# Summing v for eight blocks of queries in one go, with the exponentials' extra room taken from a third buffer of split weights

## The chip, the cores and the metric

The kernel runs on one core of one Trainium2 chip. The metric is the device time in microseconds (us) of one execution. The kernel before takes 845.59 us, the median of three runs (845.48 to 845.86).

## The reference

What must be computed, for x of 2048 rows by 512 columns in fp32, is a gated sum of two mixers:

```python
g = sigmoid((x * gate_w).sum(-1))
a = Re(DFT over the sequence of (DFT over the columns of x))   # Cr @ (x Wr') - Ci @ (x Wi')
b = softmax(q k' / 4, keys at most 255 rows back) v, 32 heads of 16 columns, then @ wo
out = g * a + (1 - g) * b
```

## The kernel before

**Two kinds of work share TensorE.** One is a stream of dense products of 128x128 weights by 512 columns: first the projections to v, q and k, then the transform over the columns (x by wi and by wr, the tile `dab`), and last, from about 300 us on, the transform over the sequence (`dc`, line 529), whose weights cr and ci come from memory in 64 pieces. Every fp32 operand of these is split into a high part `hi` (a cast) and a low part `lo` (the rest), and each product is three matmuls (hi by hi, hi by lo, lo by hi). The other kind is attention: 128 blocks of 64 queries (four groups of eight heads, 32 blocks to a group), and in each block four pairs of heads.

**The order on TensorE is written by hand** in the loop at the end of the kernel (L1020 to L1070). For each block n and each pair p it puts down: `s_pair(n, p)`, the scores (L367); a few matmuls of the dense stream (`fill`); `t_pair(k, p)`, the transposed scores of the block k = n - 19 (L449); and the dense stream again. From t, ScalarE makes exponentials (L450) into a tile PT of one block, and GpSimd zeroes what lies outside the window (L454, L458). `pv(j)` (L475) sums v with block j's exponentials: sixteen or more small matmuls, each recorded twice since fp32 takes two passes. It isn't done block by block but in *visits*: when k is at least a certain number of blocks ahead of `summed`, or at the end (k == 128), `pv` runs for all blocks from `summed` to k, and the t of that half step comes behind it. The number is 4 while the dense stream projects, and 6 once `more` is set, which happens when the projections are done ("proj"). So there are nine visits of four blocks, fifteen of six and a last one of two: 25. The other engines' order is found by the scheduler, with hints.

**Where the exponentials lie.** The pool tile `pt` has four buffers of a block each. Once `more` is set, two blocks in six go to `home` instead, a tile of 3072 columns into which projections were evicted before (`hl_tile`).

**What a visit reads and frees.** v is spread out for the matmuls by GpSimd (`v_spread`, L432) into two buffers `vpad0` and `vpad1` of four blocks each, from `vr` (one buffer), which a DMA on SyncE (SP) fills. A finished strip of 512 queries is scaled out of PSUM by VectorE (`o_out`, L496) and stored to `o_scr`.

**Pieces of cr and ci.** `Pieces.get` starts a piece: it queues the split of the next piece and loads the raw weights of the one after that, 512 KB on SP. A piece lasts 24 `dc` matmuls, and its four split jobs (L588: cast, low part, twice) are put down after the 3rd, 9th, 15th and 21st of them. `hi` and `lo` have three buffers in the pool `st`.

**The tail.** When the last visit is done, `attention_done` (L834) takes the space of `home` for a tile `rt` and that of vpad0 and vpad1 for two tiles `oraw`. The rest is the output projection by wo, in pairs of row blocks, put between the last `dc` matmuls by `tail_step` (L766): for a pair i, `wo_load` reads attention's rows back from o_scr into two `oraw` tiles, `wo_sums` makes sums on GpSimd (L876 to L879), `wo_split` splits them on ScalarE and VectorE (L80, L85), `wo_begin` starts the products (L922) with a copy on ScalarE (L931) and additions on VectorE (L933, L926), and `wo_end` finishes them. `rt` holds rows of the sequence transform, read back from `r_scr`. All loads are issued on SP, in the order of its program.

Of the kernel before, what the change touches and what calls it, by code (L numbers as in the profile page):

```python
# [32 lines left out]
def fnet_window_mix(ctx: ExitStack, tc: tile.TileContext, xT, x, wqk, wv, wr, wi, cr, ci, wo, gw, out):  # L33
    nc = tc.nc

    const = ctx.enter_context(tc.tile_pool(name="const", bufs=1))
    big = ctx.enter_context(tc.tile_pool(name="big", bufs=16))
    st = ctx.enter_context(tc.tile_pool(name="st", bufs=3))
    ev = ctx.enter_context(tc.tile_pool(name="ev", bufs=5))
    at = ctx.enter_context(tc.tile_pool(name="at", bufs=2))  # L40
    ps_a = ctx.enter_context(tc.tile_pool(name="ps_a", bufs=4, space=PSUM))
# [50 lines left out]
            mark("dve", nc.vector.scalar_tensor_tensor(lo, ps, scale, f(hi), op0=OP.mult, op1=OP.subtract))  # L92

    HALVES = slice(0, 512), slice(512, 1024)

    def load_raw(src):
        raw = st.tile([P, 1024], F32, name="raw", bufs=2)
# [1 line left out]
        return raw  # L99

    def split_raw(raw, act=False):
        hi = st.tile([P, 1024], F32R, name="hi")
        lo = st.tile([P, 1024], F32R, name="lo")
        for c in HALVES:
            split(hi[:, c], lo[:, c], raw[:, c], act)
        return hi, lo
# [2 lines left out]
    ended = []  # L109

    def split_soon(raw):
        hi = st.tile([P, 1024], F32R, name="hi")
        lo = st.tile([P, 1024], F32R, name="lo")
        for c in HALVES:
            jobs.append(lambda c=c: late(nc.scalar.copy if FIN else (nc.vector if masks else nc.gpsimd).tensor_copy,
                                         hi[:, c], raw[:, c]))
            jobs.append(lambda c=c: late((nc.vector if masks else nc.gpsimd).tensor_sub, lo[:, c], raw[:, c], f(hi[:, c])))
        return hi, lo

    def job(n):  # L120
        if n == 2 and ended:
            ended.pop(0)()
        if n % 6 == 3 and jobs:
            jobs.pop(0)()

    def load_split(src, act=False):
# [19 lines left out]

    with tc.manual_schedule(engines={mybir.EngineType.Activation, mybir.EngineType.DVE, mybir.EngineType.SP}):
        wraw, *xraw = [pt_raw() for _ in range(3)]
        wq0 = [st.tile([P, 1024], F32R, name=h) for h in ("hi", "lo")]
# [71 lines left out]
    gl = const.tile([P, 16], F32, name="gl")  # L221
    g1 = const.tile([P, 16], F32, name="g1")
    g0 = const.tile([P, 16], F32, name="g0")
    gwb = []

    GX = {}
# [10 lines left out]
    def gate(tb):  # L237
        t = GX[tb // 2][:, HALVES[tb % 2]]
        nc.vector.scalar_tensor_tensor(t, t, 1.0, gwb[0], op0=OP.mult, op1=OP.mult,
                                       accum_out=gl[:, tb:tb + 1])  # L240
        if tb == 15:
            e = const.tile([P, 16], F32, name="ge")
# [5 lines left out]
    TERMS = ((0, 0), (0, 1), (1, 0))  # L248


    home = const.tile([P, 3072], F32R, name="home")
    turn = iter(range(99))

    def hl_tile():
# [156 lines left out]
    V2 = {}  # L411
    PT = {}
    more = []

    VR = {}

# [19 lines left out]
    def t_pair(n, p):  # L436
        q0 = n % NB * BQ
        w = min(WIN, S - q0)
        if p == 0:
            if "proj" in have:  # L440
                more.append(n)
            c = (n - more[0]) % 6 * NP * WIN if more else 3072
            if c + NP * WIN <= 3072:
                PT[n] = f(home[:, c:c + NP * WIN].rearrange("p (a b) -> p a b", a=NP))
            else:
                PT[n] = at.tile([P, NP, WIN], F32, name="pt", bufs=4)
        pt = PT[n]
# [76 lines left out]
    def c_part(w, chunks, ab, ps, ends):  # L524
        for i in chunks:
            if FIN and i % 2 == 0:
                tail_step()
            for n, (a, b) in enumerate(TERMS):
                nc.tensor.matmul(ps, w[a][:, i % 8 * 128:i % 8 * 128 + 128], ab[SC[i]][:, b],  # L529
                                 start=i == ends[0] and a + b == 0, stop=i == ends[1] and a == 1)  # L530
                job(i % 8 * 3 + n + 1)
                if i != chunks[-1] or a == 0:
                    yield

# [46 lines left out]
        yield  # L581


    have = set()

    def late(fn, *args):
        with behind("act", "dve"):
# [7 lines left out]
    def dense():  # L595
# [83 lines left out]
        for sb in range(16):  # L679
# [7 lines left out]
            if sb in (5, 7):  # L687
                pieces.load()
            if sb == 11:
                pieces.split()  # L690
        for sc in range(4):
            ab[sc] = load_ab(0, sc)
# [328 lines left out]
    for n in range(N + LAG + 1):  # L1021
# [10 lines left out]
        for p in range(NP):  # L1032
            if n < N:
                s_pair(n, p)
            fill(n)
            visit = p == 0 and (k - summed >= (6 if more else 4) or k == N)
            if 0 <= k < N and not visit:
                t_pair(k, p)
            if p == 0:
# [73 lines left out]
```

## Time and profile before

| | |
|---|---|
| median of 3 runs | 845.59 us |
| the profiled execution | 845.1 us |
| its span, first to last instruction | 843.3 us |
| outside the span | 1.8 us |
| granted TensorE clock | 1.000 |
| TensorE (PE) busy | 838.5 us, 99% |
| VectorE (DVE) busy | 643.8 us, 76% |
| ScalarE (ACT) busy | 611.1 us, 72% |
| GpSimd (POOL) busy | 298.8 us, 35% |
| moved by DMA | 161.03 MB, mean 191 GB/s |

A row of a timeline gives the start in us from the span's start, the duration, the engine, the line, the operation, the tile written and those read, the form, and how many instructions the row holds; in brackets stands the idle time ahead of it and who ended it. The ends of matmuls are modelled, so of TensorE the starts are to be compared. A row of the table by windows gives a stretch, its length, then the busy time and number of instructions of PE, PE's weight loads, DVE, ACT and POOL, then the granted clock, the mean busy share of the 16 DMA engines, and GB/s.

### The profile page before, as it was taken

Reading aid. Unit: us, or ns where it says so; the run is one execution under the profiler, and the core shown is the slowest. Engines: PE = TensorE matmul, PEld = TensorE weight load, DVE = VectorE, ACT = ScalarE, POOL = GpSimd, SP = SyncE. Lnnn points to the kernel's source line nnn. Section 1 sums busy time; section 2 is a strip of 40 time slices with the busy share of each in tenths; the row PEclk is TensorE's granted clock in tenths of the full one; section 3 lists DMA queues with packets and bytes.
Section 4 is the critical chain, followed back from the end, with each engine's and each line's share of the span. In section 5 each row is a group of like instructions: output and inputs, shape, how many; then the busy total and the mean of one; then the engine's idle time right before and its main releaser. Section 6 shows DMA issues by size and latency. Waiting matters only on the chain.

```text
span 843.3 us, 17171 instructions
## 1 busy us (share of the span) xinstructions
PE 838.5 (99%) x5310; PEld 695.8 (83%) x5310; DVE 643.8 (76%) x2083; ACT 611.1 (72%) x1832; POOL 298.8 (35%) x606
## 2 busy tenths in 40 slices
PE   9999999999999999999999999999999999999998
PEld 7888888888888888888888887878887878878997
DVE  5588978677979787787877877878987867666874
ACT  6488888878888897787877977867777865553430
POOL 8102333233232233342333243343242357756410
PEclk9999999999999999999999999999999999999999
DMA  8776678485766173534454547979874256455732
GB/s 295 251 227 187 217 243 283 159 259 202 220 222 189 54 232 107 177 120 121 140 160 126 168 153 223 298 214 309 274 216 149 96 179 198 137 192 196 220 133 92
DMA packets 94475, 161.03 MB, mean 191 GB/s; under 512 B 26800, under 2 KB 35504, under 8 KB 94384
## 3 DMA queue, kind: packets, MB, share of 16 engines
q1 hardware_dynamic: 93952, 159.28, 59.1%
q8 instruction: 42, 0.69, 0.3%
q10 hardware_dynamic: 432, 0.66, 0.2%
q14 instruction: 49, 0.40, 0.1%
HBM read 108.27 MB, written 51.64 MB: 190 GB/s over the span
## 4 chain that ended last, share of the span: by engine, by line
PE 99%; DVE 1%; issue 0%; ACT 0%; DVEq 0%; ACTq 0%
PE dc L529 42%; PE dab L304 11%; PE dqk L281 10%; PE t L449 9%; PE s L367 8%; PE o L475 8%; PE dv L304 5%; PE t L922 5%; PE s L269 1%; PE dv L593 0%; PE s L387 0%; DVE pad L350 0%; PE t L559 0%; DVE sm L369 0%; ACT sm L372 0%
## 5 line engine op out<-in xcount | busy, mean ns | idle before, releaser
L529 PE MATMUL dc<-big,hi 128*128 128x512 f32 x1020 | 344.7, 393 | 0.0
L369 DVE CUSTOM_DVE_ANT_0 sm<-s,mask 128x320 f32<-128x320 f32 (+4 forms) x512 | 235.5, 465 | 111.4 <-PE s L367 71.2
L372 ACT ACTIVATE sm<-sm,ml 128x320 f32<-128x320 f32 (+4 forms) x512 | 278.2, 544 | 56.4 <-DVE ml L369 52.1
L450 ACT ACTIVATE pt<-t 128x320 f32<-128x320 f32 (+4 forms) x392 | 159.5, 411 | 83.4 <-PE t L449 78.1
L529 PE MATMUL dc<-big,lo 128*128 128x512 f32 x510 | 200.2, 393 | 0.0
L529 PEld LDWEIGHTS dc<-big,hi 128*128 128x128 f32 x1020 | 179.3, 188 | 21.4
L454 POOL TENSOR_SCALAR_AFFINE_SELECT pt<-pt 128x128 f32<-128x128 f32 x196 | 77.1, 393 | 275.0 <-ACT pt L450 273.7
L449 PE MATMUL t<-ring,pad 128*128 128x320 f32 (+4 forms) x512 | 156.8, 306 | 0.0
L367 PE MATMUL s<-ring,pad 128*128 128x320 f32 (+4 forms) x512 | 154.9, 303 | 0.1
L350 DVE TENSOR_SCALAR pad<-ring,half 96x256 fp32r<-96x256 f32 x384 | 120.0, 359 | 5.4 <-PE t L449 4.9
L449 PEld LDWEIGHTS t<-ring,pad 128*128 128x128 f32 x512 | 96.1, 188 | 30.9 <-issue 8.7
L367 PEld LDWEIGHTS s<-ring,pad 128*128 128x128 f32 x512 | 96.2, 188 | 20.6 <-DVE ml L369 0.7
L529 PEld LDWEIGHTS dc<-big,lo 128*128 128x128 f32 x510 | 95.9, 188 | 12.0
L372 ACT ACTIVATION_READ_ACCUMULATOR sm<-sm,ml 128x1 f32 x512 | 98.1, 192 | 0.0
L588 DVE TENSOR_TENSOR lo<-raw,hi 128x512 fp32r<-128x512 f32 x137 | 94.3, 696 | 2.7 <-ACT hi L588 2.5
L304 PE MATMUL dab<-hi,big 128*128 128x512 f32 x256 | 88.9, 394 | 0.0
L281 PE MATMUL dqk<-big,hi 128*128 128x512 f32 x240 | 85.0, 393 | 0.0
L432 POOL TENSOR_SCALAR vpad<-vr,half 128x256 f32<-128x256 f32 x64 | 62.2, 983 | 62.1 <-PE o L475 29.5
L348 ACT ACTIVATE pad<-ring,half 96x256 fp32r<-96x256 f32 x128 | 66.9, 522 | 0.0
L454 POOL TENSOR_SCALAR_AFFINE_SELECT home<-home 128x128 f32<-128x128 f32 x60 | 33.8, 564 | 90.2 <-ACT home L450 85.7
L458 POOL TENSOR_SCALAR_AFFINE_SELECT pt<-pt 128x128 f32<-128x128 f32 x172 | 62.9, 366 | 0.0
L588 DVE CAST hi<-raw 128x512 fp32r<-128x512 f32 x126 | 54.3, 437 | 11.3 <-PE dc L529 10.6
(122 smaller groups left out, 1034.2 us busy)
## 6 DMA issues: line engine op xcount, KB each, us to landing
qk_scr<-home SPq DMA_DIRECT2D x32, 512.0 KB
ring<-qk_scr SPq DMA_DIRECT2D x32, 512.0 KB
raw<-cr SPq DMA_DIRECT2D x32, 512.0 KB
raw<-ci SPq DMA_DIRECT2D x32, 512.0 KB
r_scr<-ev SPq DMA_DIRECT2D x42, 256.0 KB
ab_scr<-home SPq DMA_DIRECT2D x20, 512.0 KB
big<-ab_scr SPq DMA_DIRECT2D x20, 512.0 KB
ring<-qk_scr SPq DMA_DIRECT2D x32, 256.0 KB
```

The costliest lines, as they stand in the source:

```text
L281: nc.tensor.matmul(ps, w[a][:, c:c + 128], XT[dk, ss][:, b], start=n == 0, stop=n == 11)
L304: nc.tensor.matmul(ps, XT[dk, ss][:, a, c * 128:(c + 1) * 128], wh[b], start=n == 0, stop=n == 11)
L350: mark(f"pad{i}", nc.vector.tensor_scalar(dst, src, half[:96, h:h + 1], None, op0=OP.mult))
L367: nc.tensor.matmul(ps[:, :w], PAD[0, n][:, p], ring[1][:, p, k0:k0 + w], start=True, stop=True)
L369: mark("dve", nc.vector.tensor_tensor_reduce(out=sm[:, :w], in0=ps[:, :w], in1=mask[:, WIN - w:], scale=1.0, scalar=3e38, op0=OP.add, op1= ...
L372: mark("act", nc.scalar.activation(sm[:, :w], sm[:, :w], AF.Exp, bias=nm[:, c], scale=-1.0, accum_out=l[:, c]))
L449: nc.tensor.matmul(ps[:, :w], PAD[1, n][:, p], ring[0][:, p, q0:q0 + w], start=True, stop=True)
L450: nc.scalar.activation(pt[:, p, :w], ps[:, :w], AF.Exp, scale=-1.0)
L454: nc.gpsimd.affine_select(a, a, pattern=[[0, 2], [2, 64]], compare_op=OP.is_ge, fill=0.0, base=1, channel_multiplier=-1)
L475: nc.tensor.matmul(OT[g, sb][32 * p:32 * p + 32, q - sb * 512:e - sb * 512], v2[:, p], pt[:, p, q - q0:e - q0], start=first, stop=kb == 8 ...
L529: nc.tensor.matmul(ps, w[a][:, i % 8 * 128:i % 8 * 128 + 128], ab[SC[i]][:, b], start=i == ends[0] and a + b == 0, stop=i == ends[1] and a ...
L588: return fn(*args)
```

## The change

Four things are edited.

1. `st` has two buffers of each tile in place of three. `home` grows from 3072 to 5120 columns, and until the sequence transform's splits begin ("dc" in `have`, set ahead of the first `pieces.split`), every third split (`hi_lo`) takes `home`'s new columns 3072 to 5120 for its hi and lo.
2. When the projections are done, `home` is taken anew as `pth`, room for four blocks of exponentials. With the four buffers of `pt` this makes eight.
3. A visit takes eight blocks, once `more` is set and if `summed` is a multiple of 8; otherwise four.
4. The split jobs of a `dc` piece come after its 6th, 12th, 18th and 24th matmul.

```diff
-    st = ctx.enter_context(tc.tile_pool(name="st", bufs=3))
+    st = ctx.enter_context(tc.tile_pool(name="st", bufs=2))
...
+    splits = iter(range(999))
+
+    def hi_lo():
+        if "dc" not in have and next(splits) % 3 == 2:
+            return home[:, 3072:4096], home[:, 4096:5120]
+        return [st.tile([P, 1024], F32R, name=h) for h in ("hi", "lo")]
...
     def split_soon(raw):
-        hi = st.tile([P, 1024], F32R, name="hi")
-        lo = st.tile([P, 1024], F32R, name="lo")
+        hi, lo = hi_lo()
...
-    def job(n):
+    def job(n, at=3):
         if n == 2 and ended:
             ended.pop(0)()
-        if n % 6 == 3 and jobs:
+        if n % 6 == at and jobs:
             jobs.pop(0)()
...
-    home = const.tile([P, 3072], F32R, name="home")
+    home = const.tile([P, 5120], F32R, name="home")
...
         if p == 0:
             if "proj" in have:
                 more.append(n)
-            c = (n - more[0]) % 6 * NP * WIN if more else 3072
-            if c + NP * WIN <= 3072:
-                PT[n] = f(home[:, c:c + NP * WIN].rearrange("p (a b) -> p a b", a=NP))
+                if n == more[0]:
+                    pth.append(const.tile([P, 4, NP, WIN], F32, name="home", tag="home"))
+            c = (n - more[0]) % 8 if more else 4
+            if c < 4:
+                PT[n] = pth[0][:, c]
...
-                job(i % 8 * 3 + n + 1)
+                job(i % 8 * 3 + n + 1, 0)
...
             if sb == 11:
+                have.add("dc")
                 pieces.split()
...
-            visit = p == 0 and (k - summed >= (6 if more else 4) or k == N)
+            visit = p == 0 and (k - summed >= (8 if more and summed % 8 == 0 else 4) or k == N)
```

The lines of the changed kernel are numbered some nine higher: pv is L484 there, t L458, s L373, `dc` L538, and a DMA's L56 is L57. After the nine visits of four blocks, which stay, there is one more of four (to block 40), and then eleven of eight: 21 visits.

On TensorE, in the sequence transform, a visit of the kernel before stands like this in the program (names: `o` the sums, `home` and `pt` exponentials, `vpad_300` and `vpad_301` the two buffers of spread v):

```order
1552 L529 MATMUL dc<-big,hi 128x512 x2
1553 L475 MATMUL o<-pt,vpad_300 32x320 x12
1554 L475 MATMUL o<-home,vpad_300 32x320 x4
1555 L475 MATMUL o<-home,vpad_301 32x256 x4
1556 L475 MATMUL o<-home,vpad_301 32x64 x4
1557 L475 MATMUL o<-pt,vpad_301 32x192 x4
1558 L475 MATMUL o<-pt,vpad_301 32x128 x4
1559 L449 MATMUL t<-ring_265,pad_0_263 128x320
1560 L367 MATMUL s<-ring_266,pad_1_262 128x320
```

And a visit of the changed kernel:

```order
1574 L538 MATMUL dc<-big,hi 128x512
1575 L484 MATMUL o<-home,vpad_300 32x320 x12
1576 L484 MATMUL o<-pt,vpad_300 32x320 x4
1577 L484 MATMUL o<-pt,vpad_301 32x256 x4
1578 L484 MATMUL o<-pt,vpad_301 32x64 x4
1579 L484 MATMUL o<-pt,vpad_301 32x192 x4
1580 L484 MATMUL o<-pt,vpad_301 32x128 x8
1581 L484 MATMUL o<-pt,vpad_301 32x192 x4
1582 L484 MATMUL o<-home,vpad_301 32x64 x4
1583 L484 MATMUL o<-home,vpad_301 32x256 x4
1584 L458 MATMUL t<-ring_265,pad_0_263 128x320
1585 L373 MATMUL s<-ring_266,pad_1_262 128x320
```

What stands ahead of the visit (dense matmuls) and behind it (t, then s) is the same; eight blocks are summed between them in place of six, out of both vpad buffers.

On TensorE, the last visit of the kernel before sums the two blocks that are left:

```order
3046 L529 MATMUL dc<-big,lo 128x512
3047 L529 MATMUL dc<-big,hi 128x512 x2
3048 L475 MATMUL o<-pt,vpad_301 32x128 x4
3049 L475 MATMUL o<-pt,vpad_301 32x64 x4
3050 L529 MATMUL dc<-big,lo 128x512
```

In the changed kernel, at the same place between the dense matmuls:

```order
3010 L538 MATMUL dc<-big,hi 128x512 x2
3011 L484 MATMUL o<-home,vpad_300 32x320 x12
3012 L484 MATMUL o<-pt,vpad_300 32x320 x4
3013 L484 MATMUL o<-pt,vpad_301 32x256 x4
3014 L484 MATMUL o<-pt,vpad_301 32x192 x4
3015 L484 MATMUL o<-pt,vpad_301 32x128 x4
3016 L484 MATMUL o<-home,vpad_301 32x64 x4
3017 L538 MATMUL dc<-big,lo 128x512
```

The last visit now sums eight blocks, and it reads vpad0 and `home`, which the kernel before was done with one visit earlier.

On SP, around the last visit, the kernel before issues (`oraw<-o_scr_173` twice is pair 1 of the tail, its first into vpad0's space and its second into vpad1's; the four `oraw<-o_scr_176` and `oraw<-o_scr_174` are pairs 2 and 3; `rt` lies in `home`'s space; in brackets the engines and DMA queues waited for):

```order
445 L56 DMA oraw<-o_scr_173 128x4x128 [waits DMAHW2_49,PE_49]
446 L56 DMA rt<-r_scr_0_193 128x512 [waits DMAHW3_49,PE_49,Pool_49]
447 L56 DMA rt<-r_scr_1_194 128x512 [waits DMAHW4_49]
448 L56 DMA r_scr_11_204<-ev 128x512 [waits DMAHW5_49,DVE_49]
449 L56 DMA raw<-ci 128x1024 [waits DMAHW6_49,DVE_49]
450 L56 DMA oraw<-o_scr_173 128x4x128 [waits DMAHW7_49,PE_49]
451 L56 DMA rt<-r_scr_2_195 128x512 [waits DMAHW0_49]
452 L56 DMA o_scr_176<-ev 128x512 [waits DMAHW1_49,DVE_49]
453 L56 DMA rt<-r_scr_3_196 128x512 [waits DMAHW2_49]
454 L56 DMA raw<-ci 128x1024 [waits DMAHW3_49,DVE_49]
455 L56 DMA oraw<-o_scr_176 128x4x128 [waits DMAHW4_49,DMAHW1_49]
456 L56 DMA oraw<-o_scr_176 128x4x128 [waits DMAHW5_49]
```

The changed kernel issues:

```order
443 L57 DMA r_scr_11_204<-ev 128x512 [waits DMAHW1_49,DVE_49]
444 L57 DMA raw<-ci 128x1024 [waits DMAHW2_49,DVE_49]
445 L57 DMA oraw<-o_scr_173 128x4x128 [waits DMAHW3_49,PE_49]
446 L57 DMA rt<-r_scr_0_193 128x512 [waits DMAHW4_49,PE_49,Pool_49]
447 L57 DMA rt<-r_scr_1_194 128x512 [waits DMAHW5_49]
448 L57 DMA o_scr_176<-ev 128x512 [waits DMAHW6_49,DVE_49]
449 L57 DMA oraw<-o_scr_173 128x4x128 [waits DMAHW7_49]
450 L57 DMA rt<-r_scr_2_195 128x512 [waits DMAHW0_49]
451 L57 DMA rt<-r_scr_3_196 128x512 [waits DMAHW1_49]
452 L57 DMA raw<-ci 128x1024 [waits DMAHW2_49,DVE_49]
453 L57 DMA oraw<-o_scr_176 128x4x128 [waits DMAHW6_49,DMAHW3_49]
454 L57 DMA oraw<-o_scr_176 128x4x128 [waits DMAHW4_49]
```

Three loads of 256 KB each (`oraw` of pair 1's first block, `rt` 0 and 1) stood ahead of a store and of a load of ci; now they stand behind those two, next to the loads that wait for the last visit. Pair 1's two loads are 445 and 449, and those of pair 2 begin at 453.

More of the change, by code (lines that the diff above doesn't have):

```diff
@@ L36, in fnet_window_mix @@
     const = ctx.enter_context(tc.tile_pool(name="const", bufs=1))
+    have = set()
     big = ctx.enter_context(tc.tile_pool(name="big", bufs=16))
-    st = ctx.enter_context(tc.tile_pool(name="st", bufs=3))
+    st = ctx.enter_context(tc.tile_pool(name="st", bufs=2))
     ev = ctx.enter_context(tc.tile_pool(name="ev", bufs=5))
@@ L111, in split_soon @@
     def split_soon(raw):
-        hi = st.tile([P, 1024], F32R, name="hi")
-        lo = st.tile([P, 1024], F32R, name="lo")
+        hi, lo = hi_lo()
         for c in HALVES:
@@ L148, in fnet_window_mix @@
         wraw, *xraw = [pt_raw() for _ in range(3)]
-        wq0 = [st.tile([P, 1024], F32R, name=h) for h in ("hi", "lo")]
+        wq0 = hi_lo()
         zero = ev.tile([P, 512], F32R, name="ev")
@@ L223, in fnet_window_mix @@
     g0 = const.tile([P, 16], F32, name="g0")
+    ge = const.tile([P, 16], F32, name="ge")
     gwb = []
@@ L241, in gate @@
         if tb == 15:
-            e = const.tile([P, 16], F32, name="ge")
+            e = ge
             nc.scalar.activation(e, gl, AF.Exp, scale=-1.0)
@@ L413, in fnet_window_mix @@
     more = []
+    pth = []
     VR = {}
@@ L581, in c_half @@
         yield
-    have = set()
     def late(fn, *args):
```

## The prediction, made before the changed kernel was run

> **What bounds the kernel now.** I read the page's first part, then its chain of work that ended last, then TensorE's timeline at two visits. The first row gives each engine's busy time, the second the chain's shares by engine.
>
> ```profile
> PE 838.5 (99%) x5310; PEld 695.8 (83%) x5310; DVE 643.8 (76%) x2083; ACT 611.1 (72%) x1832; POOL 298.8 (35%) x606
> ...
> PE 99%; DVE 1%; issue 0%; ACT 0%; DVEq 0%; ACTq 0%
> ```
>
> TensorE is busy for 838.5 of the span's 843.3 us and it alone makes the chain. So an edit counts in two ways only: TensorE needs less time for its own order, or something makes it stand still. I therefore price the visits by the starts of TensorE's matmuls, and look for the places where another engine or a queue comes close to being late. First a visit of four blocks, from TensorE's timeline:
>
> ```profile
> 117.61 0.39 PE L304 MATMUL dab<-lo,big 128*128 128x512 f32 x1
> 117.83 0.40 PE L304 MATMUL dab<-hi,big 128*128 128x512 f32 x1
> 118.16 2.36 PE L475 MATMUL o<-pt,vpad 128*32 128x320 f32 x32
> 120.45 0.41 PE L449 MATMUL t<-ring,pad 128*128 128x320 f32 x1
> 120.70 0.30 PE L367 MATMUL s<-ring,pad 128*128 128x320 f32 x1
> ```
>
> Then one of six, and a t that no visit precedes:
>
> ```profile
> 323.01 1.84 PE L475 MATMUL o<-pt,vpad 128*32 128x256 f32 x48
> 324.66 1.26 PE L475 MATMUL o<-home,vpad 128*32 128x64 f32 x24
> 325.74 0.72 PE L475 MATMUL o<-pt,vpad 128*32 128x320 f32 x8
> 326.39 0.41 PE L449 MATMUL t<-ring,pad 128*128 128x320 f32 x1
> ...
> 327.24 0.31 PE L449 MATMUL t<-ring,pad 128*128 128x320 f32 x1
> 327.39 0.39 PE L529 MATMUL dc<-big,hi 128*128 128x512 f32 x1
> ```
>
> The reader is to see what a visit costs besides its blocks. A dense matmul starts 0.22 us after another (117.61 to 117.83), but the first sum starts 0.33 us after the last dense one (117.83 to 118.16): 0.11 us on the way in. Four blocks take 2.29 us (118.16 to 120.45) and six 3.38 (323.01 to 326.39), so a block takes (3.38 - 2.29) / 2 = 0.545, and 2.29 - 4 x 0.545 = 0.11 us belong to no block. On the way out, the s comes 0.25 us after the t (120.45 to 120.70), where a dense matmul comes 0.15 us after a t without a visit (327.24 to 327.39): 0.10 us. A visit's own price is 0.11 + 0.11 + 0.10 = **0.32 us**.
>
> **The change part by part. Fewer visits.** By the order on TensorE there are 21 in place of 25, with the same blocks and the same dense matmuls. Three of the four that go are followed by an s; one is among those after the last s, where only a t follows and the 0.10 doesn't apply. 3 x 0.32 + 0.22 = 1.18, so **-1.2 us**. Two estimates bound this: without the part that belongs to no block, -0.75; with half as much again for the switch, -1.8.
>
> A visit of eight blocks takes 8 x 0.545 + 0.11 = 4.5 us, in which TensorE makes no scores: VectorE, ScalarE and GpSimd stand for 1.1 us longer than in one of six. They are 76%, 72% and 35% busy, with the same work in total, and can catch up; nothing for it. The exponentials' eight places are all full when a visit begins, as the six were before, and the last block is read 4 us into it: nothing.
>
> **The third buffer of hi and lo.** These are the casts' waits for TensorE (total, times, longest), and the group of the low parts (total, mean ns):
>
> ```profile
> DVE hi L588 <- PE dc L529: 10.6, 6, 4.3
> ```
>
> ```profile
> L588 DVE TENSOR_TENSOR lo<-raw,hi 128x512 fp32r<-128x512 f32 x137 | 94.3, 696 | 2.7 <-ACT hi L588 2.5
> ```
>
> With two buffers, a piece's split writes where the piece before the running one lay. The change puts the first cast behind the running piece's sixth matmul, so the old reader is six matmuls (6 x 0.22 = 1.3 us) gone at that place of the order. The last low part comes behind the 24th; its half is read from the next piece's 13th matmul on, and 13 x 0.22 = 2.9 us is over four times its 0.70 us. VectorE already waits 10.6 us in six such waits, which did not make TensorE wait. So nothing; without that cover, a piece that waits for its low part would cost up to 0.7 us, on perhaps a few of 64 pieces: 0 to +2. The splits that go to the new columns of `home` are those of a few early weights, loaded long ahead, and the new `home` for exponentials is taken when the projections' evictions are done: nothing for either.
>
> **The tail.** Here the change moves loads, as the order on SP shows. Before, the last visit but one is done with vpad0 and with `home`, and three loads go out at once. These are rows of SP's timeline:
>
> ```profile
> 752.38 0.36 SPq L56 DMA_DIRECT2D oraw<-o_scr  x1
> 752.85 0.91 SPq L56 DMA_DIRECT2D rt<-r_scr  x2
> ...
> 760.30 0.37 SPq L56 DMA_DIRECT2D oraw<-o_scr  x1
> ...
> 761.31 0.38 SPq L56 DMA_DIRECT2D o_scr<-ev  x1
> ...
> 764.50 2.15 SPq L56 DMA_DIRECT2D oraw<-o_scr  x4
> ```
>
> This is the last visit, on TensorE:
>
> ```profile
> 759.63 0.54 PE L475 MATMUL o<-pt,vpad 128*32 128x128 f32 x16
> 760.09 0.50 PE L529 MATMUL dc<-big,lo 128*128 128x512 f32 x1
> ```
>
> And how full the DMA engines are, from the table by windows (the last two columns are their share and GB/s):
>
> ```profile
> 754.00:755.00 1.00, 1.00 (x6) 0.84 (x5) 0.77 (x2) 0.00 (x0) 0.29 (x1) 1.00 1.11 374
> 760.00:761.00 1.00, 1.00 (x16) 0.76 (x6) 0.69 (x1) 0.00 (x0) 0.00 (x0) 1.00 0.08 33
> 761.00:762.00 1.00, 1.00 (x6) 0.83 (x5) 0.24 (x2) 0.89 (x2) 0.00 (x0) 1.00 0.47 143
> 763.00:764.00 1.00, 1.00 (x6) 0.84 (x5) 0.62 (x2) 0.40 (x1) 0.87 (x2) 1.00 1.05 389
> 769.00:770.00 1.00, 1.00 (x6) 0.80 (x6) 0.77 (x2) 0.51 (x1) 0.23 (x1) 1.00 0.64 184
> ```
>
> The loads issued at 752 move in 754 to 756, 0.79 MB. After the change they wait for the visit that ends at the place of 760.09. Times below are counted on the scale of the kernel before, with that end in its place. `oraw` of the first block waits for vpad0 alone, free four narrow blocks (about 1 us) earlier, and falls into the stretch 760 to 761, where the engines are 0.08 busy: free. The two `rt` (0.52 MB) are issued behind the visit, from about 760.2, and take a microsecond to start moving, as the load of 752.38 does. From 761 to 762 the engines are 0.47 busy, so some 0.5 us of room is left, and after that they are full until past 769. At the 374 and 389 GB/s of full rows 0.52 MB takes 1.3 to 1.4 us, at the 311 GB/s that it shows over 754 to 756 it takes 1.7:
>
> ```profile
> 754.00:756.00 2.00, 2.00 (x12) 1.67 (x11) 1.72 (x3) 0.74 (x2) 0.29 (x1) 1.00 0.97 311
> ```
>
> I take 1.7, since these are the same loads. 1.7 - 0.5 = 1.2 us is what everything behind them in the queue comes later, pair 2's rows (the four `oraw` at 764.50) above all. The Trainium skill, DMA: Bandwidth & Descriptors, "Where 436 GB/s comes from", holds that for transfers between memory and SBUF the memory side's some 358 GB/s binds, below the ports' 435. The row of 763 to 764 with its 389 speaks against the lower figure as a bound. By the ports' figure 0.52 MB would take 1.2 us and the delay be 0.7 in place of 1.2, an estimate from that page; by 358 it would be 1.0.
>
> Who waits for pair 2's rows is seen in four engines' timelines, in the order of the chain:
>
> ```profile
> 769.77 0.74 POOL L876 TENSOR_TENSOR pt<-oraw 128x256 f32<-128x256 f32 x1 [3.50 <-PE dc L529]
> ...
> 775.94 1.43 POOL L879 TENSOR_TENSOR pt<-oraw,pt 128x256 f32<-128x256 f32 x2
> ```
>
> ```profile
> 776.71 1.05 ACT L80 CAST ring<-pt 128x1024 fp32r<-128x1024 f32 x1 [3.92 <-POOL pt L879]
> ```
>
> ```profile
> 777.80 1.36 DVE L85 TENSOR_TENSOR ring<-pt,ring 128x1024 fp32r<-128x1024 f32 x1 [2.41 <-ACT ring L80]
> ...
> 780.66 0.47 DVE L926 SCALAR_TENSOR_TENSOR rt<-t,g,rt 128x256 f32<-128x256 f32 x1
> ```
>
> ```profile
> 780.03 2.32 PE L922 MATMUL t<-ring 128*128 128x256 f32 x18
> ```
>
> GpSimd stands 3.5 us until pair 2's rows are there (TensorE is named, but the DMA engines become free just then), then ScalarE and VectorE follow without a gap. In VectorE's order the additions of pair 1 stand behind pair 2's low part, and the last of them ends at 781.13. TensorE's third product of pair 1 writes the PSUM that this addition reads: 18 matmuls in 2.32 us, so it starts at 780.03 + 12 x 0.12 = 781.47. The slack is 0.34 us, and TensorE would stand for 1.2 - 0.34 = **+0.9 us**. The bounds: 0, if the gaps take the loads in; with all three loads in front of pair 2 (0.79 MB at 311 GB/s, 2.5 us) +2.2.
>
> The sum is -1.2 + 0.9 = -0.3 us against the profiled 845.1 us (843.3 and 1.8 outside): 844.8. The median is 0.5 us above that execution, so **845.3 us**.
>
> **The rivals.** *The tail hides the loads.* GpSimd's wait speaks for a full queue, the rows of 760 to 762 for room in it. Then only the visits count: -1.2, 844.4. At the ends of the price, -0.75 and -1.8, it gives 844.8 and 843.8.
>
> *Raw weights come late: slower.* After a visit of eight, both vpad buffers are refilled, always one behind the other, through the one `vr`. On SP the second load of v waits for GpSimd's first spread, and a load of cr or ci that stands behind it waits too. SP's timeline and VectorE's show such a place, and ScalarE's how long a load takes:
>
> ```profile
> 552.22 0.37 SPq L56 DMA_DIRECT2D vr<-v_scr  x1
> ...
> 557.34 0.37 SPq L56 DMA_DIRECT2D vr<-v_scr  x1
> ...
> 562.25 0.33 SPq L56 DMA_DIRECT2D raw<-ci  x1
> ```
>
> ```profile
> 571.39 0.42 DVE L588 CAST hi<-raw 128x512 fp32r<-128x512 f32 x1
> ```
>
> ```profile
> 762.99 0.41 ACT L80 CAST ring<-oraw 128x256 fp32r<-128x256 f32 x1 [0.74 <-DMA oraw<-o_scr]
> ```
>
> Between the two loads of v lie 5.1 us. From a raw load to its cast lie 9.1 (562.25 to 571.39). 256 KB take 2.7 us from issue to use (760.30 to 762.99), so 512 KB take about 4. A raw load held up by more than 9.1 - 4 = 5.1 us makes VectorE wait in its cast; the scores' evictions are queued behind it, and TensorE waits for the PSUM they free. So it is decided at just about the hold-up seen. GpSimd comes out of a visit of eight 1.1 us later; held up 1.5 us longer than here, less the 0.7 us that the later cast gives (sixth matmul for third), a raw load would cost 0.8 us. At five of the eleven visits that is +4.0 - 0.3: 849.3; at half as many, 847.3. For it speaks that the pair of loads comes after every visit; against it, that a raw load need not stand just there in SP's order, and that eight blocks leave more time between the pairs.
>
> That the change doesn't do what it says can be left out: the order shows 21 visits.
>
> **How the numbers follow.** The forecast, both terms with a stall between 0.2 and 2.2, has 0.48; its ends are 845.6 - 1.8 + 0.2 = 844.0 and 845.6 - 0.75 + 2.2 = 847.0. The hidden tail has 0.25, the raw weights 0.20, and 0.07 is left for what I don't see. A measurement of this kernel can tell about 0.2%, 1.7 us, from no change: below 843.9 is faster, above 847.3 slower. The hidden tail is below 843.9 only near the upper price of a visit, a third of its chance (0.08); with 0.03 of the unseen that makes 0.11 faster. Slower are three quarters of the raw weights (0.15), a tail worse than its bound (0.02) and the other 0.04 of the unseen: 0.21. Within 0.2% remains 0.68. The range goes from 843.8, the hidden tail's end, to 848.2, which leaves half of the raw weights' case and the unseen outside.
>
> **What would show it.** Right: 21 visits, an s 0.25 us behind a t only after these; SP's two `rt` behind the last visit; GpSimd's first sum of pair 2 about 1.2 us later against that visit's end; a gap of about 1 us on TensorE within pair 1's second products; no new gap between 300 and 750 us. Wrong: gaps on TensorE of a microsecond after visits, with VectorE's cast waiting for a DMA into `raw` (the raw weights); no gap in the tail (hidden); low parts that TensorE waits for at a piece's 13th matmul.

## The result and the profile after

The changed kernel takes 847.93 us (median of 7 runs, 847.09 to 848.75) against 845.48 us (844.65 to 845.86): the ratio is 1.0030, with a 95% interval of 1.0019 to 1.0042, so it is 1.6 to 3.6 us slower. The forecast was 845.3 and a gain of 0.3 us. The profiled execution has a span of 846.4 us, against 843.3. From its page, the engines' busy time and the chain by engine:

```profile
PE 840.1 (99%) x5310; PEld 697.6 (82%) x5310; DVE 645.1 (76%) x2082; ACT 610.2 (72%) x1833; POOL 301.7 (36%) x606
...
PE 96%; DVE 2%; issue 1%; POOL 1%; ACT 0%; DVEq 0%; ACTq 0%
```

Two things are to be seen. The same 5310 matmuls are busy for 1.6 us longer, though there are four visits fewer; and the chain, which was 99% TensorE, now runs through VectorE and GpSimd for a few per cent: somewhere TensorE stands. Not all of the 3.1 us between these two executions belongs to the visits: 1.0 us of it is there already at the first dense matmul of the sequence transform (303.46 us before, 304.45 here), ahead of the first visit that differs. In the other traces this matmul starts at 303.6 to 303.9 with the code of before and at 303.7 to 304.2 with that of the change, so how much of it is the change's stays open.

**The visits cost what was forecast.** TensorE's timeline at a visit of eight blocks, the last of a group:

```profile
441.06 0.40 PE L538 MATMUL dc<-big,lo 128*128 128x512 f32 x1
441.38 1.82 PE L484 MATMUL o<-home,vpad 128*32 128x320 f32 x24
443.02 1.70 PE L484 MATMUL o<-pt,vpad 128*32 128x320 f32 x32
444.54 0.29 PE L484 MATMUL o<-home,vpad 128*32 128x64 f32 x8
444.76 0.41 PE L458 MATMUL t<-ring,pad 128*128 128x320 f32 x1
445.01 0.31 PE L373 MATMUL s<-ring,pad 128*128 128x320 f32 x1
```

The first sum starts 0.32 us after the dense matmul, as before, nothing waits within, and the s comes 0.25 us after the t. A visit that ends a group needs fewer sums (64 matmuls in the trace, where a block has 8 or 16, and 3.38 us); the others of eight have 96 and take 4.46 us, for which the forecast has 4.5. So four visits fewer are worth the 1.2 us of the forecast.

**The pace behind a visit.** What took them back shows in TensorE's table by windows, once one looks at the number of instructions in place of busy time. The number counts every instruction that runs in the window, also one that began ahead of it. The kernel before, between two visits:

```profile
457.00:474.00 17.00, 17.00 (x87) 14.88 (x86) 14.11 (x53) 15.30 (x48) 5.00 (x14) 1.00 0.39 130
```

The changed kernel:

```profile
457.00:474.00 17.00, 17.00 (x85) 14.45 (x85) 14.33 (x51) 15.02 (x46) 6.30 (x16) 1.00 0.31 98
```

TensorE is busy for 17.00 of 17 us in both and the clock is 1.00, but 85 matmuls run in the window in place of 87. No wait is shown. What is longer is the time from a dense matmul to the next start: 0.235 us in place of 0.228 to another dense one, 0.232 in place of 0.226 to an s or t; behind an s or t it stays 0.146. The timelines show it at the scores, which come every sixth matmul. Before:

```profile
456.25 0.31 PE L367 MATMUL s<-ring,pad 128*128 128x320 f32 x1
456.40 0.62 PE L529 MATMUL dc<-big,hi 128*128 128x512 f32 x2
456.86 0.31 PE L449 MATMUL t<-ring,pad 128*128 128x320 f32 x1
...
457.45 0.31 PE L367 MATMUL s<-ring,pad 128*128 128x320 f32 x1
```

After:

```profile
456.05 0.31 PE L373 MATMUL s<-ring,pad 128*128 128x320 f32 x1
456.20 0.63 PE L538 MATMUL dc<-big,hi 128*128 128x512 f32 x2
456.67 0.31 PE L458 MATMUL t<-ring,pad 128*128 128x320 f32 x1
...
457.28 0.31 PE L373 MATMUL s<-ring,pad 128*128 128x320 f32 x1
```

A pair's step takes 1.20 us (456.25 to 457.45) or 1.23 (456.05 to 457.28). In the sequence transform these are two clean values, 1.200 and 1.227, and one holds for a whole stretch; single steps next to a visit or to another irregular place have other lengths. The changed kernel has 24 long steps from 445.0 to 474.5 us, right behind the visit shown, up to the next place where the row of s, t and dense matmuls is broken, and 24 from 617.3 to 646.7, behind the visit at block 96. The kernel before has the second stretch only (23 steps from 616.5 to 644.7). And after the last scores, where a step is a t and three dense matmuls, 30 steps behind the visit at 694 take 0.847 in place of 0.827. That is 24 x 0.027 + 30 x 0.020 = **1.2 us** more, as much as the visits save. It fits the whole of this part: from the first dense matmul of the sequence transform to the end of the last visit the changed kernel takes 456.4 us (304.45 to 760.88), the kernel before 456.6 (303.46 to 760.09) and, in the second execution below, 456.2.

**The tail.** SP's timeline after, to be laid beside that of before:

```profile
759.93 0.37 SPq L57 DMA_DIRECT2D oraw<-o_scr  x1
761.13 1.02 SPq L57 DMA_DIRECT2D rt<-r_scr  x2
762.24 0.38 SPq L57 DMA_DIRECT2D o_scr<-ev  x1
...
766.13 0.33 SPq L57 DMA_DIRECT2D raw<-ci  x1
766.56 4.42 SPq L57 DMA_DIRECT2D oraw<-o_scr  x4
```

The table by windows shows the DMA engines (last two columns) in the last visit, at its end, and later:

```profile
758.00:759.00 1.00, 1.00 (x20) 0.51 (x16) 0.00 (x0) 0.00 (x0) 0.00 (x0) 1.00 0.00 0
...
760.00:761.00 1.00, 1.00 (x33) 0.76 (x26) 0.00 (x0) 0.00 (x0) 0.00 (x0) 1.00 0.07 19
...
762.00:763.00 1.00, 1.00 (x6) 0.84 (x5) 0.00 (x0) 0.00 (x0) 0.00 (x0) 1.00 0.92 170
...
770.00:771.00 1.00, 1.00 (x6) 0.81 (x5) 0.32 (x1) 1.00 (x3) 0.60 (x1) 1.00 1.14 342
```

The last visit's end, on TensorE:

```profile
760.66 0.29 PE L484 MATMUL o<-home,vpad 128*32 128x64 f32 x8
760.88 0.50 PE L538 MATMUL dc<-big,lo 128*128 128x512 f32 x1
```

And the chain that follows, on GpSimd, ScalarE, VectorE and TensorE:

```profile
773.17 1.05 POOL L885 TENSOR_TENSOR pt<-oraw 128x256 f32<-128x256 f32 x1 [2.57 <-PE t L931]
```

```profile
779.96 1.05 ACT L81 CAST ring<-pt 128x1024 fp32r<-128x1024 f32 x1 [6.42 <-POOL pt L888]
780.92 0.36 ACT L940 COPY pt<-t 128x256 f32<-128x256 f32 x1
```

```profile
783.88 0.47 DVE L935 SCALAR_TENSOR_TENSOR rt<-t,g,rt 128x256 f32<-128x256 f32 x1
```

```profile
781.34 0.97 PE L931 MATMUL t<-ring 128*128 128x256 f32 x6 [0.36 <-ACT pt L940]
783.18 0.97 PE L931 MATMUL t<-ring 128*128 128x256 f32 x6 [0.87 <-DVE rt L935]
784.41 0.98 PE L931 MATMUL t<-ring 128*128 128x256 f32 x6 [0.26 <-DVE rt L935]
```

The last visit ends at 760.88 here, at 760.09 before. While it lasts the DMA engines stand still; then everything comes at once and they are full from 762 to 771. GpSimd's first sum of pair 2 starts 773.17 - 760.88 = 12.29 us behind that end, before it was 769.77 - 760.09 = 9.68: **2.6 us** later. TensorE's second products of pair 1, one row of 18 before, fall into three with gaps ahead of each, and from the visit's end to the last dense matmul TensorE needs **2.3 us** more: the 2.6 less the slack of 0.34.

What holds pair 2's loads back on SP is seen one row ahead of them. The load of ci at 766.13 must wait until VectorE has read the piece that lay in its place, and VectorE reads it late:

```profile
764.21 0.69 DVE L86 TENSOR_TENSOR ring<-oraw,ring 128x512 fp32r<-128x512 f32 x1 [2.42 <-ACT ring L81]
764.82 1.28 DVE L596 TENSOR_TENSOR lo<-raw,hi 128x512 fp32r<-128x512 f32 x2
```

The low parts end at 766.10, and the load goes out at once. They stand behind the split of pair 1's rows, which came late themselves; in the kernel before the same two low parts end at 763.05, ahead of that split. (How long the store to `o_scr` alone would have held pair 2's loads isn't shown.) So pair 2's loads go out 5.7 us behind the visit's end in place of 4.4. The other half of the 2.6 us arises after their issue, while the DMA engines are full: 6.6 us from there to GpSimd's first sum, in place of 5.3.

### The profile page after: what moved, and what is told of

It is laid out like the page before. It is cut to its first block, busy times and chain, and to the rows that moved or that the text cites. A ratio compares the mean times of both kernels' runs of the same rounds, so it can differ in the third digit from the quotient of the medians.

```text
span 846.4 us, 17177 instructions
## 1 busy us (share of the span) xinstructions
PE 840.1 (99%) x5310; PEld 697.6 (82%) x5310; DVE 645.1 (76%) x2082; ACT 610.2 (72%) x1833; POOL 301.7 (36%) x606
## 4 chain that ended last, share of the span: by engine, by line
PE 96%; DVE 2%; issue 1%; POOL 1%; ACT 0%; DVEq 0%; ACTq 0%
PE dc L538 41%; PE dab L310 11%; PE t L458 9%; PE dqk L287 9%; PE s L373 8%; PE o L484 8%; PE dv L310 5%; PE t L931 4%; PE s L275 1%; PE dv L601 0%; DVE sm L375 0%; DVE pad L356 0%; POOL pt L886 0%; POOL pt L887 0%; DVE home L91 0%
## 5 line engine op out<-in xcount | busy, mean ns | idle before, releaser
L538 PE MATMUL dc<-big,hi 128*128 128x512 f32 x1020 | 344.9, 394 | 0.0
L538 PE MATMUL dc<-big,lo 128*128 128x512 f32 x510 | 200.6, 393 | 0.0
L538 PEld LDWEIGHTS dc<-big,hi 128*128 128x128 f32 x1020 | 179.0, 188 | 21.3
L459 ACT ACTIVATE pt<-t 128x320 f32<-128x320 f32 (+4 forms) x332 | 134.9, 409 | 35.0 <-PE t L458 32.7
L463 POOL TENSOR_SCALAR_AFFINE_SELECT pt<-pt 128x128 f32<-128x128 f32 x166 | 66.5, 401 | 252.5 <-ACT pt L459 252.4
L458 PE MATMUL t<-ring,pad 128*128 128x320 f32 (+4 forms) x512 | 156.2, 305 | 0.0
L373 PE MATMUL s<-ring,pad 128*128 128x320 f32 (+4 forms) x512 | 155.2, 303 | 0.1
L458 PEld LDWEIGHTS t<-ring,pad 128*128 128x128 f32 x512 | 96.1, 188 | 29.1 <-issue 7.1
L373 PEld LDWEIGHTS s<-ring,pad 128*128 128x128 f32 x512 | 96.1, 188 | 21.5 <-DVE ml L375 1.4
L459 ACT ACTIVATE home<-t 128x320 f32<-128x320 f32 (+1 forms) x180 | 73.5, 411 | 55.4 <-PE t L458 54.7
L538 PEld LDWEIGHTS dc<-big,lo 128*128 128x128 f32 x510 | 95.9, 188 | 12.7
L439 POOL TENSOR_SCALAR vpad<-vr,half 128x256 f32<-128x256 f32 x64 | 65.8, 1040 | 80.2 <-PE o L484 23.7
L596 DVE TENSOR_TENSOR lo<-raw,hi 128x512 fp32r<-128x512 f32 x134 | 92.0, 694 | 1.3 <-ACT hi L596 1.3
L463 POOL TENSOR_SCALAR_AFFINE_SELECT home<-home 128x128 f32<-128x128 f32 x90 | 42.1, 468 | 89.5 <-ACT home L459 86.4
L310 PE MATMUL dab<-home,big 128*128 128x512 f32 x192 | 62.8, 394 | 0.0
L596 DVE CAST hi<-raw 128x512 fp32r<-128x512 f32 x122 | 52.4, 436 | 6.8 <-PE dc L538 6.8
```

The source lines that it names most:

```text
L310: nc.tensor.matmul(ps, XT[dk, ss][:, a, c * 128:(c + 1) * 128], wh[b], start=n == 0, stop=n == 11)
L373: nc.tensor.matmul(ps[:, :w], PAD[0, n][:, p], ring[1][:, p, k0:k0 + w], start=True, stop=True)
L458: nc.tensor.matmul(ps[:, :w], PAD[1, n][:, p], ring[0][:, p, q0:q0 + w], start=True, stop=True)
L459: nc.scalar.activation(pt[:, p, :w], ps[:, :w], AF.Exp, scale=-1.0)
L463: nc.gpsimd.affine_select(a, a, pattern=[[0, 2], [2, 64]], compare_op=OP.is_ge, fill=0.0, base=1, channel_multiplier=-1)
L596: return fn(*args)
```

## Experiments

Their times stand against runs of the kernel before made on the same chip at the same time. Three theories were to be told apart. *Queue*: the loads that now stand behind the last visit make TensorE wait in the tail. *Buffers*: two buffers of split weights, or weights that lie in `home`, slow the dense matmuls. *Pace*: where a visit falls decides between the two steps. The third grew out of the two steps of the dense matmuls, which show when the traces before and after are laid beside each other, and at first stood only as "by chance".

**The tail alone, in the kernel before.**

```diff
-            visit = p == 0 and (k - summed >= (6 if more else 4) or k == N)
+            visit = p == 0 and (k - summed >= (6 if more and summed % 6 == 2 else 2 if summed == 36 else 4) or k == N)
```

> The kernel before with its visit of two blocks moved from the end to the start of the sequence transform (at block 38), so that the last visit sums six blocks (122 to 127) and frees vpad0 and home only at the end; as many visits as before, three buffers of split weights. Queue theory (three loads of the tail now stand behind the last visit, pair 2's rows come later, TensorE waits in pair 1's second products): 1.5 to 2.5 us slower than the kernel before, GpSimd's first sum of pair 2 about 2 us later against the last visit's end. Rival, that the loss lies in the buffers of split weights: no change, 845.5.

Measured: 847.0 against 845.49 us, ratio 1.0019 (1.0010 to 1.0028), 1.5 us slower. Pair 2's four loads go out at 766.57, 6.6 us behind the last visit's end (4.4 in the kernel before), and the stretch behind that visit takes 1.3 us more. A loss in the tail is there with three buffers and as many visits: the queue makes it, not the buffers. But it doesn't lie where it was expected. Pair 2's first sum comes 1.3 us later and not 2, and TensorE loses 0.3 us in pair 0's second products, 0.7 in pair 1's first and only 0.2 in pair 1's second: here pair 1's rows are late too (their first sum 5.3 us behind the visit's end, 3.0 before). The pace changes with the visits in this run as well: no long steps at 616 to 645 us, but 22 of 0.847 behind the visit at 711.

**The buffers alone, with visits of six.**

```diff
-            c = (n - more[0]) % 8 if more else 4
-            if c < 4:
+            c = (n - more[0]) % 6 if more else 4
+            if c < 2:
...
-            visit = p == 0 and (k - summed >= (8 if more and summed % 8 == 0 else 4) or k == N)
+            visit = p == 0 and (k - summed >= (6 if more else 4) or k == N)
```

> The changed kernel with visits of six again (25 visits, a last one of two, as in the kernel before); the split weights keep two buffers, the third split in home, and the later split jobs. Queue theory: the last visit of two gives the loads back, so no wait in the tail, 845.5 as the kernel before. Buffer theory (the dense matmuls run slower where split weights lie in home or have two buffers): 1 to 2 us slower than the kernel before, with more stretches in which a dense matmul takes 0.235 in place of 0.228 us. If such stretches fall by chance: 845.5 with their usual spread.

Measured: 846.05 against 845.49, ratio 1.0010 (1.0001 to 1.0019), 0.1 to 1.6 us slower; the long steps stand where the kernel before has them (23 from 617 to 645 us), and the tail takes 78.5 us, between the 78.2 and 78.7 of two executions of the kernel before. From the sequence transform's first dense matmul to the last visit's end it takes 456.4 us, also between theirs. So the trace shows no place where the buffers cost anything; the runs leave 0.1 to 1.6 us open.

**The loads out early again.** The changed kernel with the shift of one block in `home` and a last visit cut in two:

```diff
-            c = (n - more[0]) % 8 if more else 4
+            c = (n - more[0] - 1) % 8 if more else 4
...
-            visit = p == 0 and (k - summed >= (8 if more and summed % 8 == 0 else 4) or k == N)
+            visit = p == 0 and (k - summed >= (6 if summed == 120 else 8 if more and summed % 8 == 0 else 4) or k == N)
```

> The changed kernel with home's exponentials shifted by one block (blocks 120 to 123 in home, 124 to 127 in pt) and its last visit cut in two: six blocks at 126 and two at the end, so 22 visits. Queue theory: the three loads go out early, the 2.3 us of standing in the tail go and one visit (0.3 us) comes back: 2.0 us faster than the changed kernel, 845.9; if the dense stretches are chance, 844.6. Buffer theory: no more than 0.3 us from the changed kernel, 847.5 to 848.2.

Measured: 846.39 against 845.49, ratio 1.0014 (1.0005 to 1.0022). TensorE's second products of pair 1 are one row again:

```profile
780.54 2.31 PE L931 MATMUL t<-ring 128*128 128x256 f32 x18
```

The standing in the tail is gone to the last tenth, and yet three visits fewer than before leave 0.9 us of loss (0.4 to 1.9 by the interval). So the tail isn't all. The trace has the long steps from 444 to 474 us that the changed kernel has.

**The shift alone.** The first of the two edits above, without the second.

> The changed kernel with home's exponentials shifted by one block, so that the last visit is done with home after its first four blocks, about a microsecond before its end; still 21 visits. Queue theory: the two loads into rt go out a microsecond earlier, into a stretch in which the DMA engines stand still, so about 1 us of the 2.3 us in the tail goes: 846.8. Buffer theory: as the changed kernel, 847.9.

Measured: 847.43, ratio 1.0022 (1.0012 to 1.0032): half a microsecond from the changed kernel, which the runs don't tell from none. The expectation failed in an instructive way. The two `rt` did go out earlier (759.59), but both loads of pair 1 and another `rt` then stood ahead of the store to `o_scr`, which left at 763.05, 2.6 us behind the visit's end (1.2 in the kernel before, 1.4 in the changed one). Pair 2's rows are read from what this store writes, and their loads could go only at 768.12. (The Trainium skill, DMA: Bandwidth & Descriptors, "Rules for kernel authors", asks that a DMA that reads what an earlier one wrote wait for its completion; this kernel does: SP stands for the store for 3.7 us here and 1.0 in the kernel before, while in the changed kernel no such wait is shown, since the load of ci holds SP longer.) And the loss moved to another place:

```profile
770.18 0.96 DVE L86 TENSOR_TENSOR ring<-pt,ring 128x768 fp32r<-128x768 f32 x1 [2.20 <-ACT ring L81]
```

```profile
772.26 0.98 PE L931 MATMUL t<-ring 128*128 128x256 f32 x6 [0.24 <-DVE rt L935]
```

VectorE stands until pair 1's sums can be split, with pair 0's additions behind the split in its order, and TensorE loses 1.1 us in pair 0's second products, 0.7 in pair 1's first and 0.2 in pair 1's second. A load put ahead of others only moved the wait.

**Pair 2 ahead of rt.**

```diff
-        r_load(0)
         wo_load(1)
-        r_load(1)
-        for i in range(2, 4):
-            wo_load(i)
+        wo_load(2)
+        r_load(0)
+        r_load(1)
+        wo_load(3)
```

> The changed kernel with the two loads of pair 2's rows issued ahead of the four loads into rt. Queue theory: 1 MB less stands ahead of pair 2's rows, GpSimd's first sum of pair 2 comes 2 us or more earlier against the last visit's end, and the 2.3 us of standing in pair 1's second products shrink to under 0.7, unless the later rt makes VectorE wait: 846.0 to 846.8. If the rows are late for another reason (their own store, which they read back): 847.9 as the changed kernel.

Measured: 846.24 against 845.46, ratio 1.0008 (0.9999 to 1.0016), 1.7 us faster than the changed kernel by the two medians, which come from different sets of runs. SP's timeline, GpSimd's and TensorE's:

```profile
761.48 0.36 SPq L57 DMA_DIRECT2D o_scr<-ev  x1
765.02 0.91 SPq L57 DMA_DIRECT2D oraw<-o_scr  x2
766.03 1.88 SPq L57 DMA_DIRECT2D rt<-r_scr  x4
```

```profile
768.95 0.77 POOL L885 TENSOR_TENSOR pt<-oraw 128x256 f32<-128x256 f32 x1 [0.86 <-DMA oraw<-o_scr]
```

```profile
780.66 2.32 PE L931 MATMUL t<-ring 128*128 128x256 f32 x18
```

Both loads of pair 1 go first (759.60), then the store, pair 2 and only then `rt`. Pair 2's first sum comes 8.4 us behind the visit's end (12.3 in the changed kernel, 9.7 before), the gaps on TensorE are gone, and the tail takes 78.4 us (80.5 and 78.2). So the order of the loads on SP makes the loss in the tail; which of the moved loads it is isn't told, since pair 1's and pair 2's were moved together.

**A last visit of four.** The shift of one block, and visits that end at 44, 52 to 124 and 128:

```diff
-            visit = p == 0 and (k - summed >= (8 if more and summed % 8 == 0 else 4) or k == N)
+            visit = p == 0 and (k - summed >= (8 if summed >= 36 else 4) or k == N)
```

> The changed kernel with its visits of eight ending at blocks 44, 52 to 124 in place of 48 to 128, so that the last visit sums only four blocks (21 visits as in the changed kernel), and home's exponentials shifted by one block so that home is free at block 124. Queue theory: the three loads go out one visit early, no wait in the tail (2.3 us gone). Pace theory (TensorE's step of one pair takes 1.200 or 1.227 us over long stretches, and where the visits fall in a group of 32 blocks decides which): the slow stretch of 440 to 477 us, which all kernels with visits ending at multiples of 8 showed, moves or goes. Both right and no new slow stretch: 845.5 - 1.3 = 844.2. If the slow stretch stays (0.8 us): 845.0. If the loss lies elsewhere: 846 to 847.5.

Measured: 847.88 against 845.46, ratio 1.0030 (1.0018 to 1.0041): above every number expected. The long steps moved (395 to 418 and 654 to 678 us) and did not go. And here raw weights came late, as in the forecast's slower rival. VectorE's and TensorE's timelines:

```profile
532.68 0.43 DVE L596 CAST hi<-raw 128x512 fp32r<-128x512 f32 x1 [1.95 <-DMA raw<-cr]
...
541.80 0.43 DVE L596 CAST hi<-raw 128x512 fp32r<-128x512 f32 x1 [2.48 <-DMA raw<-cr]
```

```profile
542.68 0.41 PE L373 MATMUL s<-ring,pad 128*128 128x320 f32 x1 [1.21 <-DVE ml L375]
```

Two raw pieces of cr came late. VectorE stood for 2.0 and 2.5 us ahead of the casts, and TensorE's steps at these two places are 0.7 and 1.5 us longer in all. What made the pieces late was not followed; the nearest pair of loads of v went out at 509 us. In the changed kernel's trace no cast waits for a raw piece.

**Both kernels profiled again.**

> The kernel before, profiled once more. Pace theory, with the stretches set by the order of the program: slow steps of a pair (1.227 us) at 480 to 488 and 610 to 650 us again and at no other place. If they fall by chance: other stretches.

> The changed kernel, profiled once more. Pace theory, with the stretches set by the order of the program: slow steps of a pair (1.227 us) at 440 to 477 and 610 to 650 us again. If they fall by chance: other stretches, and another span.

Measured: 845.35 and 846.98. The long steps at 616 to 645 and at 445 to 474 us came back in both as the order has them, so they are no chance. A few others did not (480 to 483 us in the kernel before; one stretch of 272 to 291 us, behind the same visit, comes and goes in runs with the same order up to there; it is short in the first trace of the kernel before and long in that of the changed kernel, 15 x 0.027 = 0.4 us of the 1.0 by which the latter is late at 304 us). The tail differs by execution: from block 128 on the changed kernel lost 2.3 us in the first profile and 0.6 in the second, first against first and second against second, from the last visit's end to the last dense matmul. Pair 2's first sum came 2.6 us later in the first pair and 0.6 in the second (10.86 us behind the visit's end against 10.25).

**The pace set anew.** `fill` runs one dense matmul more ahead of a t and one less behind it, in the block after the visits at 64, 96 and 112:

```diff
+            nudge = p == 0 and k in (65, 97, 113)
+            quota += nudge
             fill(n)
+            quota -= nudge
```

> The changed kernel with pair 2's rows loaded ahead of rt, as in the run before, and one dense matmul moved ahead of a t at three places: in the first block after the visits that end at blocks 64, 96 and 112, behind which TensorE kept a longer step (1.227 for 1.200 us of a pair, and 0.847 for 0.827 after the last scores). Pace theory, with the pace a state that any irregular place sets anew: the steps behind these three places fall back to 1.200 and 0.827, worth 26 x 0.027 + 26 x 0.027 + 30 x 0.020 = 2.0 us: 844.3 against the 846.2 of the run without the move. If the longer steps have a lasting reason (loads, other engines, the place of the operands): no change from 846.2, the steps as long as before.

> The kernel before with one dense matmul moved ahead of a t in the first block after the visit that ends at block 96, its one visit in the sequence transform with steps of 1.227 us behind it. Pace theory, with the pace a state that any irregular place sets anew: 24 x 0.027 = 0.65 us faster, 844.8. If the longer steps have a lasting reason: 845.5, steps as before.

Measured: 845.17 against 845.74, ratio 0.9994 (0.9985 to 1.0003), for the changed kernel with pair 2 ahead; 1.2 us less than without the move, by the two ratios, which leave it open by about 1 us. The expectation had 2.0. The kernel before with one move: 845.44, ratio 0.9997 (0.9988 to 1.0006), no difference that the runs tell from the 0.65 expected or from none. The table by windows for the first:

```profile
457.00:474.00 17.00, 17.00 (x87) 14.86 (x86) 14.65 (x53) 15.38 (x47) 5.55 (x15) 1.00 0.38 120
```

and for the kernel before without and with the move, behind the visit at block 96:

```profile
622.00:644.00 22.00, 22.00 (x109) 18.72 (x109) 19.80 (x67) 19.30 (x59) 8.47 (x22) 1.00 0.46 154
```

```profile
622.00:644.00 22.00, 22.00 (x112) 19.19 (x111) 20.45 (x69) 19.31 (x61) 8.70 (x22) 1.00 0.48 160
```

At all four places the steps fall to 1.200 (and 0.827) right at the move, some five steps behind the visit: 87 matmuls again in place of 85, and 112 in place of 109. Behind the move the order on TensorE is the same as without it, so the pace is a state that a break in the row sets and not a lasting cost of loads, operands or other engines. The gain is smaller than expected in part because a new stretch came: 15 steps of 0.847 behind the visit at 725, where the changed kernel has none.

**One move more**, behind that visit, which ends at block 120.

> The run before with one more moved matmul, behind the visit that ends at block 120, after which the run before kept steps of 0.847 us for 15 steps. Pace theory: those steps fall to 0.827, 15 x 0.020 = 0.3 us: about 844.9 against the kernel before's 845.5 to 845.7, and still 21 visits. If the pace is chance: 845.2 as the run before.

Measured: 845.56 against 845.64, ratio 0.9997 (0.9988 to 1.0006). The 0.847 there did fall to 0.827, but the tail of this profile took 0.4 us more than in the run before, and the runs tell no gain. Of these last two versions neither is shown to beat the kernel before; both beat the changed one.

## Why the prediction was wrong

- **Fewer visits, -1.2 us.** Right: the way in, the way out and the blocks have the forecast's durations.
- **The visits' cover ("nothing for it").** This step failed, and it decided the sign with the tail. A visit was priced at 0.32 us by what stands between the dense matmul before it and the s behind it, and what it leaves behind was put at nothing. The forecast looked for engines that must catch up; what came was a step of 1.227 in place of 1.200 us for the next 30 us, on TensorE itself. The kernel before shows both values in its own trace (23 steps of 1.227 from 616.5 to 644.7 us), and the forecast read two visits and no step behind them. By the steps it is +1.2 us, which takes back what the visits save. The moves show that the long steps cost time, 1.2 us by the runs; they acted on three stretches, one of which the kernel before has too, so the equal number is chance. Why TensorE keeps one of two paces stays open.
- **The third buffer, nothing.** Open. The run with visits of six leaves 0.1 to 1.6 us for the buffers and the later split jobs together, and its trace shows no place for them.
- **The tail, +0.9 us.** The path was right for the changed kernel, from the order on SP to TensorE's second products of pair 1, and the slack of 0.34 fits the first profile (2.6 - 0.34 = 2.3). The mis-sized term is the delay of pair 2's rows, 1.2 us: it measured 2.6 in one execution, just above the 2.5 of the forecast's upper bound, and 0.6 in the other. Two reasons show in the rows. The load that was to be free found the DMA engines idle, but went out at 759.93 and moved only behind 761. And the delay was worked out from bytes in a queue alone, where pair 1's late rows also made VectorE free a raw piece late, and the load of ci that waited for it stood ahead of pair 2. The changed order of the loads gave back 1.7 us.
- **The raw weights (the slower rival).** Not in the changed kernel. The kernel with visits at 44 to 124 shows that raw pieces can come late; whether by the pair of loads of v and beyond 5.1 us, as the forecast had it, was not tested.
- **The sum.** -1.2 + 1.2 + 0.6 to 2.3 = +0.6 to +2.3 us by the two pairs of profiles, and +1.7 with what the runs give for the tail, at the low end of the measured 1.6 to 3.6; the rest is not placed. With the loads and the three matmuls moved, the same 21 visits go from a ratio of 1.0030 to 0.9994, 3.0 us less, which is more than the loss. The range held the time, the sign was wrong.

## What to carry to other kernels

Price a break in a regular row of matmuls by the steps behind it too: lay the starts of one recurring matmul side by side, or compare the number of instructions in long windows, since "busy 100%" is the same at both paces. When a buffer's last reader moves, list every load that waits for it, and then every load queued behind those, with what it waits for in its turn: here a late load made another engine free a buffer late, and the queue stood for that. Three moved matmuls and a new order of loads were each worth as much here as the four visits.

## What the hardware showed that I had not expected

TensorE runs the same row of six matmuls in 1.200 or in 1.227 us (four in 0.827 or 0.847), with each start behind a dense matmul later (0.235 in place of 0.228 us between two dense ones in the row of six), at a granted clock of 1.00 and with no wait shown. The value is set where the row is broken, is the same in repeated executions at most places, and holds until the next break; a single matmul put one place earlier was enough to change it at four places.
